# Convolution and gate kernel on one core: in blocks 27 to 33 the product of chunk 2 goes from VectorE to GpSimd, with ScalarE evicting it first

## The chip, the cores and the metric

The kernel runs on one core of one Trainium2 chip. The metric is the time of one execution on the device, in microseconds; the time of before is the median of three runs.

A core has five engines that run their own queues of instructions strictly in order and wait for each other with semaphores: TensorE (PE, with its weight loads as PEld) for matrix products, VectorE (DVE), ScalarE (ACT) and GpSimd (POOL) for elementwise work, and SyncE (SP), which here only issues DMAs. TensorE writes to PSUM; here VectorE and ScalarE read it from there.

## What is computed

```python
def _attn_ref(x, weight):                 # x (8, 4224, 192), weight (8, 7)
    w = softmax(weight, axis=-1)          # one 7-tap filter per head, 8 heads of 24 channels
    # causal convolution along the sequence, one filter for the 24 channels of a head
    out = np.einsum('hk,bskhg->bshg', w, x_unf)

def _moe_ref(x, w_val, conv_w, w_out):    # x is the result above
    for k in range(5):                    # causal, one 5-tap filter for each channel
        gate_pre += conv_w[k][None, None, :] * xp[:, k:k + S, :]
    gate = 1.0 / (1.0 + np.exp(-gate_pre))
    val = x @ w_val                       # 192 x 192
    return gate * val @ w_out             # 192 x 192
```

## The kernel before, in words

**Layout.** The eight sequences are laid end to end as two halves of four. Channels lie on the partitions and tokens on the free axis. 192 channels are one and a half times 128 partitions, so three chunks are worked on: chunks 0 and 1 are the first 128 channels of the two halves of the batch, held together as one tile with 2 x 502 columns, and chunk 2 is the other 64 channels of both halves, stacked into 128 partitions, 502 columns.

**Groups and blocks.** The tokens are cut into 14 groups (NJS), and the groups into 36 blocks (STEPS, numbered n = 0 to 35). Most blocks have 502 tokens of each half; blocks 32 and 33 have 448, block 34 has 500 and block 35 has 188. The last block of the loop, n = 36, only finishes block 35.

**The first convolution** is a product with a banded matrix on TensorE. Its work is cut into units (`conv_unit`): four matrix products into one PSUM bank (pc, L318), one copy by ScalarE (e, L327), and, where a head is complete, DMAs on SP's queue that scatter the result into the group's x tiles (L356) and issue the next loads of the input (L167). Units are run two groups ahead: the list `todo` says how many units run at the end of each block. Group 12 (blocks 32 and 33) and group 13 (blocks 34 and 35) are the last.

**A block** has these steps, in the shorthand of the code:

- `split(n+1)`: x of the next block is split into a rounded part and a remainder, since TensorE multiplies rounded values. ScalarE casts (xh, L418 for chunks 0 and 1, L426 for chunk 2) and GpSimd subtracts (xl, L419 and L427).
- v = x @ w_val on TensorE, in parts: `diagonal` (L453), `main` (L463), `columns` (L491), `rows` (L476). Chunk 2 of v is finished by `columns`, chunks 0 and 1 by `rows`.
- the gate of a coming block. For chunks 0 and 1 together (tile pa) and for chunk 2 (tile pb), ScalarE opens an accumulator in PSUM with the first tap (`gate_open`, L390), VectorE adds taps 1 to 4 one after the other (`gate_taps`, L397), and ScalarE closes it with the sigmoid (`gate_close`, L410) into the tile g. There is one accumulator for each, so the next block's opening comes right after the closing.
- `gated(n, q)`: g times v for chunk q, from the PSUM bank of v, in place in g (L510, VectorE).
- `split_gated1(n)` and `split_gated2(n)`: the product is split again for the second matrix product: ScalarE casts (ph), GpSimd subtracts (pl).
- o = (g v) @ w_out, one block behind: the products of block n-1 are made during block n, and `project(n-1, q)` copies each bank out (ot, L526) to be stored.

**PSUM.** The accumulators of the gate have banks of their own. All else, v, o and pc, takes five banks in turn (pool `ps`). In a block the order of taking is v chunk 2, o chunk 2, v chunk 0, v chunk 1, o chunk 0, o chunk 1, then one for each unit of the convolution. So o chunk 1 takes the bank of v chunk 2 of the same block; it can start when that is read.

**The order of the work** is written out by hand: every engine runs its instructions in the order of the calls. The main loop (L636 to L675) calls the steps above. VectorE's taps are the part that can be shifted: a block must have done a number of them (`ahead(n)`) ahead of its own gate, eight per block plus a lead that the table LEAD gives (4 taps in blocks 19 to 27, then 3, 2, 1 and 0). Taps ahead of `gated(n, 2)` are here called the first part, those that the second `while` adds, up to a cost of FITS, the second. When the last tap of an accumulator is done, `flush` puts its closing and the next opening on ScalarE's queue: at the next tap of the same kind, or at one of the calls of `flush` in the loop. If the last tap of chunks 0 and 1 falls in the second part, up to two convolution units are put ahead of that closing.

Of the kernel before, what the change touches and what calls it, by code (L numbers as in the profile page):

```python
# [7 lines left out]
F32 = mybir.dt.float32  # L8
# [4 lines left out]
ALU = mybir.AluOpType  # L13
# [47 lines left out]
NG = len(NJS)  # L61
# [7 lines left out]
STEPS = []  # L69
# [5 lines left out]
N = len(STEPS)  # L75
LAST = N - 1
MB = 502
# [19 lines left out]

LEAD = {0: 0, 10: 1, 13: 2, 16: 3, 19: 4, 28: 3, 30: 2, 32: 1, 33: 0}  # L100
BETWEEN = {9, 12, 15, 18}
COST, FITS = (1.3, 0.78), 4.6

SOON = {2: (0, 2), 3: (1, 3), 4: (3, 5), 5: (5, 8)}

# [2 lines left out]
def kernel(  # L108
# [9 lines left out]
    nc = tc.nc  # L118
# [5 lines left out]
    gp = ctx.enter_context(tc.tile_pool(name="gp", bufs=3))  # L124
    pp = ctx.enter_context(tc.tile_pool(name="pp", bufs=2))
    op = ctx.enter_context(tc.tile_pool(name="op", bufs=3))
    ps_g = ctx.enter_context(tc.tile_pool(name="ps_g", bufs=1, space=PSUM))
    ps_h = ctx.enter_context(tc.tile_pool(name="ps_h", bufs=1, space=PSUM))
    ps = ctx.enter_context(tc.tile_pool(name="ps", bufs=5, space=PSUM))
# [51 lines left out]
    def scratch(n, i):  # L181
        o = scr_at[i]
        scr_at[i] += n
        return scr[i][:, o : o + n].bitcast(I32)

    raw = {}
    for name, ap, n, i in (("wv", wv, 2 * D + 2 * KG, 2), ("wo", wo, 2 * D, 1)):
        t = scratch(2 * n, i)
# [182 lines left out]
    def views(n, k=KG - 1):  # L371
        g, o, m = STEPS[n]
        b = second(NJS[g])
        x1v = x1s[g][:, : 2 * b].rearrange("p (a t) -> p a t", a=2)
        return x1v[:, :, o + k : o + k + m], x2s[g][:, o + k : o + k + m]
# [3 lines left out]
    accs, g1s, g2s, xs, pr, ots, banks = {}, {}, {}, {}, {}, {}, {}  # L379

    def gate_open(n, i):
        if n >= N:
            return
        m = STEPS[n][2]
        if i == 0:
            acc = ps_g.tile([128, 2, 512], F32, tag="pa", name=f"pa_{n}")[:, :, :m]
        else:
            acc = ps_h.tile([128, 512], F32, tag="pb", name=f"pb_{n}")[:, :m]
        accs[n, i] = acc
        nc.scalar.mul(acc, views(n, 0)[i], cwt[:, i, 0:1])  # L390
# [11 lines left out]
    def gate_close(n, i):  # L402
        if n >= N:
            return
        m = STEPS[n][2]
        if i == 0:
            dst = g1s[n] = gp.tile([128, 2, MB], F32, tag="g1", name=f"g1_{n}")[:, :, :m]
        else:
            dst = g2s[n] = gp.tile([128, MB], F32, tag="g2", name=f"g2_{n}")[:, :m]
        nc.scalar.activation(dst, accs.pop((n, i)), AF.Sigmoid)  # L410
# [11 lines left out]
    def split2(pool, tag, n, x):  # L422
        m = STEPS[n][2]
        h = pool.tile([128, MB], F32R, tag="h2", name=f"{tag}h2_{n}")[:, :m]
        l = pool.tile([128, MB], F32R, tag="l2", name=f"{tag}l2_{n}")[:, :m]
        nc.scalar.copy(h, x)  # L426
        nc.gpsimd.tensor_tensor(out=l, in0=x, in1=h.bitcast(F32), op=ALU.subtract)  # L427
        return h, l
# [3 lines left out]
    def bank(what, n, q):  # L432
        t = ps.tile([128, 512], F32, tag="p", name=f"{what}_{n}_{q}")[:, : STEPS[n][2]]
        banks[what, n, q] = t
        return t

    def operands(what, n):
        return (w_val, *xs[n, 1], *xs[n, 2]) if what == "v" else (w_out, *pr[n, 1], *pr[n, 2])

    def parts(w, h, l):  # L440
        return (w.h, h), (w.l, h), (w.h, l)

    def ok(n):
        return 0 <= n < N

    def diagonal(what, n):
        if not ok(n):
            return
        acc = bank(what, n, 2)
        w, _, _, h2, l2 = operands(what, n)  # L450
        r = slice(W22, W22 + 128)
        for i, (a, b) in enumerate(parts(w, h2, l2)):
            nc.tensor.matmul(acc, lhsT=a[:, r], rhs=b, start=(i == 0), stop=False)  # L453

    def main(what, n, q):
        if not ok(n):
            return
        fresh = (what, n, q) not in banks
        acc = bank(what, n, q) if fresh else banks[what, n, q]
        w, h, l, _, _ = operands(what, n)  # L460
        r = slice(W11, W11 + 128)
        for i, (a, b) in enumerate(parts(w, h, l)):
            nc.tensor.matmul(  # L463
                acc, lhsT=a[:, r], rhs=b[:, q], start=(fresh and i == 0), stop=(not fresh and i == 2)
            )

    def rows(what, n):
        if not ok(n):
            return
        fresh = (what, n, 0) not in banks  # L470
        two = [bank(what, n, q) if fresh else banks[what, n, q] for q in range(2)]
        w, _, _, h2, l2 = operands(what, n)
        r = slice(W21, W21 + 128)
        for i, (a, b) in enumerate(parts(w, h2, l2)):
            for acc, p in zip(two, HALVES):
                nc.tensor.matmul(  # L476
                    acc, lhsT=a[p, r], rhs=b[p], start=(fresh and i == 0), stop=(not fresh and i == 2)
                )

    def columns(what, n):  # L480
        if not ok(n):
            return
        m = STEPS[n][2]
        acc = banks[what, n, 2]
        w = w_val if what == "v" else w_out
        x = views(n)[0] if what == "v" else g1s[n]
        cuts = [m * i // 4 for i in range(5)]
        for i in range(4):
            c = slice(cuts[i], cuts[i + 1])
            for q, p in enumerate(HALVES):  # L490
                nc.tensor.matmul(  # L491
                    acc[p, c], lhsT=w.f[:, W12 : W12 + 64], rhs=x[:, q, c],
                    start=False, stop=(i == 3),
                )

    def split(n):
        if n >= N:
            return
        x1, x2 = views(n)
        if n == 0:  # L500
            xs[n, 2] = split2(sp, "x", n, x2)
        xs[n, 1] = split1(sp, "x", n, x1)
        if n > 0:
            xs[n, 2] = split2(sp, "x", n, x2)

    def gated(n, q):
        if not ok(n):
            return
        v = g1s[n][:, q] if q < 2 else g2s[n]
        nc.vector.tensor_tensor(out=v, in0=banks.pop(("v", n, q)), in1=v, op=ALU.mult)  # L510

    def split_gated1(n):
# [3 lines left out]
    def split_gated2(n):  # L516
        if ok(n):
            pr[n, 2] = split2(pp, "p", n, g2s[n])

    def project(n, q):  # L520
        if not ok(n):
            return
        m = STEPS[n][2]
        if n not in ots:
            ots[n] = op.tile([128, 3 * MB], F32, tag="ot", name=f"ot_{n}")
        nc.scalar.copy(ots[n][:, q * m : (q + 1) * m], banks.pop(("o", n, q)))  # L526
        o = 3 * sum(s[2] for s in STEPS[:n])
        if n == LAST:
            nc.sync.dma_start(out[:, o + q * m : o + (q + 1) * m], ots[n][:, q * m : (q + 1) * m])
        elif q == 1:  # L530
            nc.sync.dma_start(out[:, o : o + 3 * m], ots[n][:, : 3 * m])
# [16 lines left out]
    for g in range(LAG, NG):  # L548
        a, b = SOON.get(g) or (first[g - LAG], first[g - 1])
        if g == NG - 1:  # L550
            a, b = a - 1, b - 1
        k = first_unit[g + 1] - first_unit[g]
        for i in range(k):
            todo[a + i * (b - a) // k] += 1
# [63 lines left out]
    def flush(*which):  # L618
        for n, i in [p for p in pending if p[1] in which]:
            gate_close(n, i)  # L620
            gate_open(n + 1, i)
            pending.remove((n, i))
# [9 lines left out]
    def ahead(n):  # L632
        lead = LEAD[max(k for k in LEAD if k <= n)]
        return min(2 * T * (n - HEAD) + T + lead, len(taps))

    for n in range(HEAD, N + 1):  # L636
        diagonal("v", n)
        split(n + 1)
        diagonal("o", n - 1)
        main("v", n, 0)  # L640
        main("v", n, 1)
        while at_tap[0] < ahead(n):
            tap()
        columns("v", n)
        gated(n, 2)
        flush(0)
        columns("o", n - 1)
        split_gated2(n)
        project(n - 1, 2)
        rows("v", n)  # L650
        if n in BETWEEN:
            tap()
        gated(n, 0)
        gated(n, 1)
        rows("o", n - 1)
        split_gated1(n)
        flush(1)
        main("o", n - 1, 0)
        used = first_used = 0
        while at_tap[0] < ahead(n + 1):  # L660
            _, i, k = taps[at_tap[0]]
            if used + COST[i] > FITS:
                break
            used += COST[i]
            tap()
            if (i, k) == (0, T):
                first_used = used
        project(n - 1, 0)
        main("o", n - 1, 1)
        project(n - 1, 1)  # L670
        now = min(todo[n], 2 if first_used else 0)
        conv(now)
        flush(0)
        conv(todo[n] - now)
        flush(1)  # L675
# [91 lines left out]
```

## Time and profile before

| What | Value |
|---|---|
| Median of 3 runs | 390.35 us (389.66 to 391.41) |
| Profiled execution | 390.87 us |
| Its span in the profile | 388.7 us |
| TensorE busy | 375.8 us, 97% of the span |
| VectorE busy | 340.8 us, 88% |
| ScalarE busy | 327.4 us, 84% |
| GpSimd busy | 254.6 us, 66% |
| Granted TensorE clock, mean | 0.992 |

The profile is of one execution. Its span lies a little below that execution's own time, the rest being what lies around the traced instructions. Rows that group instructions give the line, the engine, the operation, what is written from what, the number of instructions, and then busy time in us, the mean in ns of one, and the idle time of the engine just before them with what ended it. Rows of the order of time give the start in us, the length in us, the engine, the line and the operation; in brackets stands how long the engine had been idle and what it had waited for. Where instructions of one engine overlap a little, the distance of two starts is what one of them costs.

### The profile page before, as it was taken

How to read it: one execution, taken by the hardware profiler on the slowest of the kernel's cores; microseconds unless marked ns; L12 is line 12 of the kernel's file. 1: busy time of each engine (PE TensorE's matmuls, PEld its weight loads, DVE VectorE, ACT ScalarE, POOL GpSimd, SP SyncE). 2: the span in 40 equal slices, each digit the busy share in tenths (PEclk: the TensorE clock that was granted, in tenths of full speed). 3: DMA queues.
4: the chain of work that ended last, by engine and by line, in shares of the span. 5: the costliest groups of instructions: out<-in, count | busy, mean ns of one | idle time of the engine just before them, and what ended most of it. 6: DMA issues, size and time to landing. Idle time of an engine off the chain costs nothing.

```text
span 388.7 us, 8631 instructions
## 1 busy us (share of the span) xinstructions
PE 375.8 (97%) x3204; PEld 321.0 (83%) x3204; DVE 340.8 (88%) x424; ACT 327.4 (84%) x525; POOL 254.6 (66%) x177
## 2 busy tenths in 40 slices
PE   8798999999999999999999999999999999999895
PEld 8697988988888888888888888888888788887784
DVE  4769899888999999999999999899899988999970
ACT  7568888989888889889988988888888889987863
POOL 1869765556667765666665766776566675777771
PEclk9989999999999999999999999999999999999998
DMA  8887869999788689687867668768887736342223
GB/s 297 235 207 228 249 216 288 255 271 223 227 247 237 197 244 230 211 236 239 244 197 237 201 193 257 206 198 260 249 234 209 242 128 215 124 147 80 81 103 149
DMA packets 38209, 82.49 MB, mean 212 GB/s; under 512 B 4856, under 2 KB 17528, under 8 KB 38168
## 3 DMA queue, kind: packets, MB, share of 16 engines
q1 hardware_dynamic: 36720, 79.90, 68.4%
q0 software_dynamic: 896, 1.31, 1.4%
q10 hardware_dynamic: 552, 0.73, 0.6%
q8 instruction: 25, 0.41, 0.5%
q14 instruction: 16, 0.13, 0.1%
HBM read 29.34 MB, written 26.00 MB: 142 GB/s over the span
## 4 chain that ended last, share of the span: by engine, by line
PE 86%; DVE 6%; DMA 3%; ACT 2%; issue 1%; SPq 1%; DVEq 0%; ACTq 0%
PE pc L318 22%; PE o L463 13%; PE v L463 11%; PE v L491 8%; PE v L476 7%; PE o L491 7%; PE o L476 6%; PE o L453 5%; PE v L453 5%; DVE pa L397 3%; DVE g L510 2%; DMA x<-xw 2%; DVE pb L397 1%; PE pw L210 1%; SPq L356 1%
## 5 line engine op out<-in xcount | busy, mean ns | idle before, releaser
L397 DVE SCALAR_TENSOR_TENSOR pa<-x,cwt,pa 128x1004 f32<-128x1004 f32 (+5 forms) x144 | 172.8, 1200 | 9.5 <-ACT pa L390 5.6
L419 POOL TENSOR_TENSOR xl<-x,xh 128x1004 fp32r<-128x1004 f32 (+5 forms) x36 | 74.7, 2075 | 80.3 <-ACT xh L418 69.1
L318 PEld LDWEIGHTS pc<-band,x 128*120 128x120 f32 x912 | 102.8, 187 | 5.8 <-issue 3.4
L318 PE MATMUL pc<-band,x 128*120 128x122 f32 x912 | 103.8, 272 | 3.2 <-DMA x<-xw 3.2
L397 DVE SCALAR_TENSOR_TENSOR pb<-x,cwt,pb 128x502 f32<-128x502 f32 (+5 forms) x144 | 102.2, 710 | 3.9 <-ACT pb L390 0.7
L419 POOL TENSOR_TENSOR pl<-g,ph 128x1004 fp32r<-128x1004 f32 (+5 forms) x36 | 79.1, 2197 | 21.4 <-ACT ph L418 19.2
L510 DVE TENSOR_TENSOR g<-v,g 128x502 f32<-128x502 f32 (+5 forms) x108 | 65.8, 642 | 21.0 <-PE v L476 16.4
L327 ACT COPY e<-pc 120x488 f32<-120x488 f32 x114 | 61.3, 576 | 13.0 <-PE pc L318 11.9
L526 ACT COPY ot<-o 128x502 f32<-128x502 f32 (+5 forms) x108 | 55.9, 547 | 3.3 <-PE o L463 2.6
L427 POOL TENSOR_TENSOR pl<-g,ph 128x502 fp32r<-128x502 f32 (+5 forms) x36 | 43.4, 1204 | 13.4 <-ACT ph L426 13.1
L418 ACT CAST ph<-g 128x1004 fp32r<-128x1004 f32 (+5 forms) x36 | 35.2, 979 | 14.7 <-DVE g L510 14.6
L410 ACT ACTIVATE g<-pa 128x1004 f32<-128x1004 f32 (+5 forms) x36 | 34.7, 965 | 10.7 <-DVE pa L397 9.9
L427 POOL TENSOR_TENSOR xl<-x,xh 128x502 fp32r<-128x502 f32 (+5 forms) x36 | 41.8, 1161 | 0.0
L390 ACT ACTIVATE pa<-x,cwt 128x1004 f32<-128x1004 f32 (+5 forms) x36 | 37.8, 1050 | 2.5 <-DMA x<-e 1.4
L491 PEld LDWEIGHTS v<-x,wvf 128*64 128x64 f32 x576 | 29.1, 136 | 11.8 <-issue 11.4
L491 PE MATMUL v<-x,wvf 128*64 128x125 f32 (+4 forms) x576 | 37.2, 270 | 0.0
L491 PE MATMUL o<-g,wof 128*64 128x125 f32 (+4 forms) x576 | 35.5, 264 | 0.0
L418 ACT CAST xh<-x 128x1004 fp32r<-128x1004 f32 (+5 forms) x36 | 35.2, 978 | 0.0
L491 PEld LDWEIGHTS o<-g,wof 128*64 128x64 f32 x576 | 30.9, 136 | 0.1
L463 PE MATMUL o<-ph,woh 128*128 128x502 f32 (+5 forms) x72 | 30.9, 429 | 0.0
L463 PE MATMUL v<-xh,wvh 128*128 128x502 f32 (+5 forms) x72 | 27.2, 377 | 0.3 <-ACT e L327 0.3
L463 PE MATMUL o<-ph,wol 128*128 128x502 f32 (+5 forms) x72 | 27.2, 377 | 0.0
(75 smaller groups left out, 567.4 us busy)
## 6 DMA issues: line engine op xcount, KB each, us to landing
x<-xw SPq DMA_DIRECT2D x64, 300.0 KB
out<-ot SPq DMA_DIRECT2D x24, 753.0 KB
x<-e SPq DMA_DIRECT2D x40, 285.9 KB
x<-xw SPq DMA_DIRECT2D x20, 360.0 KB
out<-ot SPq DMA_DIRECT2D x8, 672.0 KB
x<-e SPq DMA_DIRECT2D x32, 141.6 KB
x<-e SPq DMA_DIRECT2D x25, 171.6 KB
x<-e SPq DMA_DIRECT2D x16, 94.4 KB
```

Source lines behind the costliest of these rows:

```text
L318: nc.tensor.matmul(pc[:M, k * WIN : (k + 1) * WIN], lhsT=xtiles[i][:, c : c + M], rhs=band[:, 4 * q + hi, :], start=True, stop=True,)
L327: nc.scalar.copy(e[:, a : a + w], pc[:M, :w])
L397: nc.vector.scalar_tensor_tensor(out=acc, in0=views(n, k)[i], scalar=cwt[:, i, k : k + 1], in1=acc, op0=ALU.mult, op1=ALU.add,)
L418: nc.scalar.copy(h, x)
L419: nc.gpsimd.tensor_tensor(out=l, in0=x, in1=h.bitcast(F32), op=ALU.subtract)
L427: nc.gpsimd.tensor_tensor(out=l, in0=x, in1=h.bitcast(F32), op=ALU.subtract)
L453: nc.tensor.matmul(acc, lhsT=a[:, r], rhs=b, start=(i == 0), stop=False)
L463: nc.tensor.matmul(acc, lhsT=a[:, r], rhs=b[:, q], start=(fresh and i == 0), stop=(not fresh and i == 2))
L476: nc.tensor.matmul(acc, lhsT=a[p, r], rhs=b[p], start=(fresh and i == 0), stop=(not fresh and i == 2))
L491: nc.tensor.matmul(acc[p, c], lhsT=w.f[:, W12 : W12 + 64], rhs=x[:, q, c], start=False, stop=(i == 3),)
L510: nc.vector.tensor_tensor(out=v, in0=banks.pop(("v", n, q)), in1=v, op=ALU.mult)
L526: nc.scalar.copy(ots[n][:, q * m : (q + 1) * m], banks.pop(("o", n, q)))
```

## The change

Four things change. In blocks 27 to 33 (ASIDE) chunk 2's product is made by GpSimd: ScalarE copies the bank of v into a new tile in SBUF (vt, one buffer), and GpSimd multiplies it with g. In these blocks the call of `gated(n, 2)` moves behind `flush(0)`, and the call of `split_gated2(n)` moves behind `project(n-1, 2)`. The lead is five taps in blocks 27 to 31, three in block 32 and none from block 33. And group 12's six units run in blocks 26 and 27, three each, where they ran in blocks 26, 27 and 28, two each; block 28 keeps the two units of group 13.

```diff
-LEAD = {0: 0, 10: 1, 13: 2, 16: 3, 19: 4, 28: 3, 30: 2, 32: 1, 33: 0}
+LEAD = {0: 0, 10: 1, 13: 2, 16: 3, 19: 4, 27: 5, 32: 3, 33: 0}
+
+ASIDE = range(27, N - 2)
...
+    vp = ctx.enter_context(tc.tile_pool(name="vp", bufs=1))
...
         v = g1s[n][:, q] if q < 2 else g2s[n]
+        if q == 2 and n in ASIDE:
+            t = vp.tile([128, MB], F32, tag="vt", name=f"vt_{n}")[:, : STEPS[n][2]]
+            nc.scalar.copy(t, banks.pop(("v", n, q)))
+            nc.gpsimd.tensor_tensor(out=v, in0=t, in1=v, op=ALU.mult)
+            return
         nc.vector.tensor_tensor(out=v, in0=banks.pop(("v", n, q)), in1=v, op=ALU.mult)
...
         if g == NG - 1:
             a, b = a - 1, b - 1
+        if g == NG - 2:
+            b = b - 1
...
         columns("v", n)
-        gated(n, 2)
+        if n not in ASIDE:
+            gated(n, 2)
         flush(0)
+        if n in ASIDE:
+            gated(n, 2)
         columns("o", n - 1)
-        split_gated2(n)
+        if n not in ASIDE:
+            split_gated2(n)
         project(n - 1, 2)
+        if n in ASIDE:
+            split_gated2(n)
         rows("v", n)
```

With the new leads, the taps by block are as follows (28a4 is the fourth tap of block 28's chunks 0 and 1, 28b1 the first of its chunk 2):

```
block  first part                     second part
27     28a4 28b1-28b4 29a1            29a2 29a3 29a4
28     29b1-29b4 30a1                 30a2 30a3 30a4
29     30b1-30b4 31a1                 31a2 31a3 31a4
30     31b1-31b4 32a1                 32a2 32a3 32a4
31     32b1-32b4 33a1                 33a2 33a3 33a4
32     33b1-33b3                      33b4 34a1 34a2
33     34a3 34a4                      34b1-34b4 35a1
```

Before, block 27 had 28a4 28b1-28b4 and then 29a1-29a3, block 28 had 29a4 29b1-29b3 and then 29b4 30a1 30a2, and so on, so that the last tap of chunks 0 and 1 always stood in the first part.

## The prediction

> **What bounds the kernel now.** I read the page first (busy shares and the chain that ended last), then the stretches block by block, then each engine's order of time in blocks 27 to 35.
>
> ```profile
> span 388.7 us, 8631 instructions
> PE 375.8 (97%) x3204; PEld 321.0 (83%) x3204; DVE 340.8 (88%) x424; ACT 327.4 (84%) x525; POOL 254.6 (66%) x177
> PE 86%; DVE 6%; DMA 3%; ACT 2%; issue 1%; SPq 1%; DVEq 0%; ACTq 0%
> ```
>
> TensorE sets the time, and it stops doing so only where VectorE carries 6% of the chain. A block starts at its first diagonal product of v; cut at these starts, blocks 26 to 34 are:
>
> ```profile
> 293.75:303.18 9.43, 9.43 (x81) 7.80 (x80) 8.81 (x11) 8.18 (x13) 5.83 (x5) 1.00 0.87 248
> 303.18:313.54 10.36, 9.94 (x82) 7.87 (x80) 10.11 (x13) 9.19 (x15) 7.51 (x5) 1.00 0.58 187
> 313.54:324.66 11.12, 11.12 (x98) 9.47 (x96) 10.14 (x12) 9.47 (x15) 7.68 (x5) 1.00 0.56 194
> 324.66:334.15 9.49, 9.49 (x82) 7.84 (x80) 8.09 (x11) 8.53 (x13) 5.57 (x4) 1.00 0.41 125
> 334.15:343.55 9.40, 9.40 (x82) 7.79 (x80) 8.82 (x11) 8.61 (x14) 6.91 (x5) 1.00 0.39 139
> 343.55:351.63 8.08, 8.08 (x66) 6.29 (x65) 7.69 (x11) 7.05 (x11) 5.75 (x4) 1.00 0.47 163
> 351.63:360.15 8.52, 7.83 (x64) 6.08 (x62) 8.37 (x11) 6.87 (x12) 6.31 (x4) 1.00 0.23 91
> 360.15:368.66 8.51, 7.43 (x64) 6.01 (x62) 8.34 (x10) 6.58 (x12) 6.49 (x5) 1.00 0.23 93
> 368.66:376.10 7.44, 7.44 (x64) 6.07 (x63) 6.54 (x12) 5.38 (x11) 5.71 (x5) 1.00 0.23 92
> ```
>
> The columns are the length, then busy time of PE, PEld, DVE, ACT and POOL, the granted clock (1.00 throughout) and the DMAs. A block with two convolution units is 9.43 us of PE work (26, 29, 30); four units make 11.12, so a unit is 0.84. Block 27 has two units and takes 10.36: 0.93 lost. Block 31, without units, should take 9.40 - 1.68 = 7.72 and takes 8.08: 0.36. Blocks 32 and 33 do no more than block 34 (7.44) and take 1.08 and 1.07 longer. That is 3.4 us, and the rows say who has it:
>
> ```profile
> 309.58 0.49 PE L476 MATMUL o<-ph,woh 64*128 64x502 f32 x1 [0.42 <-DVE g L510]
> 357.82 0.49 PE L476 MATMUL o<-ph,woh 64*128 64x502 f32 x1 [0.69 <-DVE g L510]
> 366.52 0.47 PE L476 MATMUL o<-ph,woh 64*128 64x448 f32 x1 [1.08 <-DVE g L510]
> ```
>
> The second accumulator of "rows o" takes the PSUM bank of v chunk 2, which VectorE frees only when its queue reaches `gated(n, 2)`. This is what the change attacks.
>
> **The change, part by part.** *VectorE loses* seven products:
>
> ```profile
> L510 DVE TENSOR_TENSOR g<-v,g 128x502 f32<-128x502 f32 x72 | 46.5, 675 | 12.1 <-PE v L476 11.6 <-PE v L491 0.4
> L427 POOL TENSOR_TENSOR pl<-g,ph 128x502 fp32r<-128x502 f32 x24 | 30.6, 1277 | 7.7 <-ACT ph L426 7.4
> L427 POOL TENSOR_TENSOR xl<-x,xh 128x502 fp32r<-128x502 f32 x24 | 29.0, 1210 | 0.0
> L419 POOL TENSOR_TENSOR pl<-g,ph 128x1004 fp32r<-128x1004 f32 x24 | 55.9, 2329 | 16.4 <-ACT ph L418 14.8 <-DMA x<-e 0.6 <-PE o L463 0.6
> L419 POOL TENSOR_TENSOR xl<-x,xh 128x1004 fp32r<-128x1004 f32 x24 | 51.6, 2148 | 60.8 <-ACT xh L418 55.8 <-DMA x<-e 5.0
> ```
>
> 7 x 0.675 = 4.7 us off VectorE's queue, which was what PE waited for. With PE bound everywhere the most this can return is the 3.4 us above. *The convolution units* only move: block 26 gets a third (starting 27 at 303.18 + 0.84 = 304.02), block 27 a third, block 28 drops to two. The sum for PE is 0, and so is that of their copies and scatter DMAs; these leave SP's queue earlier. Their cover is PE's work on other blocks' data; if a scatter landed late it would cost the wait of ScalarE's opening for block 32, at the earliest one block later, so I take 0.
>
> *ScalarE and GpSimd gain* seven copies and seven products, and here the order matters more than the sum. In an ASIDE block ScalarE's queue is: cast xh, cast xh2 (block n+1); copy of v; one output copy; **cast ph2, which needs GpSimd's product**; cast ph; close and open of chunk 2; two output copies; two convolution copies; close and open of chunks 0 and 1; next block's xh. GpSimd's is: xl, xl2 (they need xh, xh2), **product**, pl2, pl. So cast ph2 waits until GpSimd has done xl, xl2 and the product, these wait for cast xh, and the next cast xh is behind cast ph2. That is a closed loop, once round per block; before, ph2 waited for VectorE and no loop ran through GpSimd. Its price, from block 28 (times are starts; the distance of two starts is the cost):
>
> ```profile
> 313.83 1.05 ACT L327 COPY e<-pc 120x488 f32<-120x488 f32 x2
> 314.75 1.06 ACT L418 CAST xh<-x 128x1004 fp32r<-128x1004 f32 x1
> 315.68 0.64 ACT L426 CAST xh<-x 128x502 fp32r<-128x502 f32 x1
> 316.19 1.04 ACT L410 ACTIVATE g<-pa 128x1004 f32<-128x1004 f32 x1
> 317.26 1.10 ACT L390 ACTIVATE pa<-x,cwt 128x1004 f32<-128x1004 f32 x1
> 318.61 0.61 ACT L426 CAST ph<-g 128x502 fp32r<-128x502 f32 x1 [0.24 <-DVE g L510]
> 319.13 0.57 ACT L526 COPY ot<-o 128x502 f32<-128x502 f32 x1
> 320.68 1.03 ACT L418 CAST ph<-g 128x1004 fp32r<-128x1004 f32 x1 [0.98 <-DVE g L510]
> 321.62 1.05 ACT L526 COPY ot<-o 128x502 f32<-128x502 f32 x2
> 322.56 1.26 ACT L327 COPY e<-pc 120x488 f32<-120x488 f32 x2
> ...
> 325.39 0.60 ACT L410 ACTIVATE g<-pb 128x502 f32<-128x502 f32 x1
> 326.02 0.69 ACT L390 ACTIVATE pb<-x,cwt 128x502 f32<-128x502 f32 x1
> 326.64 1.02 ACT L418 CAST xh<-x 128x1004 fp32r<-128x1004 f32 x1
> ```
>
> ```profile
> 315.89 2.15 POOL L419 TENSOR_TENSOR xl<-x,xh 128x1004 fp32r<-128x1004 f32 x1 [1.66 <-ACT xh L418]
> 318.00 1.28 POOL L427 TENSOR_TENSOR xl<-x,xh 128x502 fp32r<-128x502 f32 x1
> 319.36 1.28 POOL L427 TENSOR_TENSOR pl<-g,ph 128x502 fp32r<-128x502 f32 x1
> ```
>
> GpSimd's leg: 314.75 to 315.89 is 1.14 from xh's start to xl's, xl 2.11, xl2 1.28, the product 1.28 (not in the trace; the same width and operand count as xl2), 0.05 of hand-over: 5.86. The copy of v (0.57 by the output copies' row) and two neighbours hide in it; uncovered, seven copies would cost 4.0. ScalarE's leg: ph2 0.52, ph 0.94, close 0.63 and open 0.62, two output copies 0.94, two convolution copies 0.92, close 1.07, open 1.10: 6.74. Once round: **12.6 us, against 9.43 of PE work.**
>
> The lead belongs to this sum. With the leads of before, the last tap of chunk 0 falls ahead of the gate, and its close and open (2.17) run while GpSimd is at xl. With five taps it falls after the convolution copies, so both stand in ScalarE's leg, ahead of the next cast xh; queued behind them are the two casts and everything GpSimd does.
>
> The older limit of before is that xh starts at block start plus 1.2 (314.75 - 313.54). PE can stand a lag only until it needs the next bank: with two units the next diagonal product of o takes the bank of o chunk 0, freed by an output copy 5.86 + 0.52 + 0.94 + 1.25 + 0.57 = 9.1 after xh's start. PE wants it 9.43 + 0.7 = 10.1 after the block's start. So the slack is used up when xh starts 1.0 into the block; every further turn of the loop is paid in full.
>
> **The sum.** The casts xh by block, from these rows:
>
> ```profile
> 304.91 1.06 ACT L418 CAST xh<-x 128x1004 fp32r<-128x1004 f32 x1
> ...
> 346.50 2.11 POOL L419 TENSOR_TENSOR xl<-x,xh 128x896 fp32r<-128x896 f32 x1 [1.70 <-DMA out<-ot]
> 348.56 1.16 POOL L427 TENSOR_TENSOR xl<-x,xh 128x448 fp32r<-128x448 f32 x1
> ...
> 371.52 0.49 ACT L418 CAST xh<-x 128x376 fp32r<-128x376 f32 x1
> ```
>
> Block 27: 304.91 + 0.46 (a third convolution copy of block 26) = 305.37. Its leg through GpSimd ends at 311.23; ScalarE's 6.74 and a third convolution copy (0.46) bring xh of block 28 to 318.43, which is 4.1 into a block that starts at 304.02 + 10.3 = 314.3. From there 12.6 each for blocks 28 and 29, and 12.4 for block 30, whose close and opens are already of 448: 331.0, 343.6, 356.0. Block 31 has no convolution copies and narrower x: GpSimd 1.0 + 2.06 + 1.16 + 1.28 + 0.05 = 5.55, ScalarE 6.74 - 0.92 - 0.25 = 5.57, together 11.1: 367.1. In blocks 32 and 33 fewer taps are ahead, and chunk 0's close and open are out of ScalarE's leg: 5.45 + 3.45 = 8.9 and 5.85 + 3.2 = 9.05 (outputs of 448): 385.0 for the cast that was at 371.52. Block 34 is gated by VectorE again, and the rest runs as before. The lag is 385.0 - 371.5 = 13.5 us.
>
> The profiled execution took 390.87 (span 388.7), 0.52 over the median of the runs, 390.35. 390.87 + 13.5 = 404.4, on the median's footing **403.9**. A shift of this kind already holds VectorE's gain: with PE and ScalarE late, VectorE is never late.
>
> *Bounds.* Product at VectorE's own price (0.675), xl2 at its mean (1.21): the loop is 11.9, and six such turns take 4 off: 400. Product 8% dearer, as pl stands to xl among the wide rows (2329 to 2148), and 0.14 for each hand-over, as 319.36 stands to the end of cast ph2 (318.61 + 0.61): 0.4 a turn, 2.5 more: 406.5. I take 1.28, as GpSimd's two-input subtractions at that width all lie between 1.21 and 1.28 on the group rows.
>
> [...]
>
> **The rivals.**
> (a) *Faster.* The loop doesn't bite and the VectorE waits vanish: 390.35 - 3.4 = 387.0. It needs ScalarE's ph2 to find the product ready, so GpSimd to be through xl and xl2 before v is. For it: GpSimd is busy only 5.6 to 7.7 us a block. Against it: the order of the queues; share of busy time says nothing of a loop. It decides where a turn is below 9.43, 3.2 less than the rows give.
> (b) *Half of it.* PE's slack and shorter legs take part of the lag, turns of about 11: 404 - 6 x 1.5 = 395. For it: the 5-bank rotation can reach further than I walked. Against: the slack was 0 in block 28 already.
> (c) *No change.* ScalarE's extra 4.0 us replaces VectorE's 3.4 us as a plain load: 391.
> (d) *Clock.* PE idles about 2.3 us at a time (block 29: at 324.5 + 0.7 against a bank freed near 327.5); if the clock fell, the 9.43 of PE work would double in places and join the loop: 408 to 415. Against: 1.08 us of wait left the granted clock at 1.00 in block 33, and nothing longer stands in these blocks.
> [...]
>
> **How the numbers follow.** My forecast 0.74, (a) 0.08, (b) 0.09, (c) 0.04, (d) 0.05. What a measurement here can tell is about 0.5%, 2 us. Faster is (a), 0.08; same is (c), 0.04; the rest, 0.88, is slower. The range 396 to 410 takes my forecast with both bounds, the upper half of (b) and the start of (d).
>
> **What would show it.** Right: ScalarE's cast ph2 (L426) waits 2 to 3 us for the new GpSimd product in blocks 28 to 31; xh to xh is about 12.5 us there; PE waits for ScalarE's output copies at the diagonal product of o (L453), not for L510. Blocks 26 and before are unchanged but for one unit. Wrong: GpSimd's product starts as soon as the copy of v lands, xh stays near 1.2 us into its block, or block lengths stay near 9.4.

## The result, and the profile after

The changed kernel takes 401.9 us (median of 6 runs, 400.36 to 403.76); the kernel before takes 389.6 us in the same comparison. The ratio is 1.0303, with a 95% interval of 1.0273 to 1.0332: 12.3 us slower, where 13.5 were forecast. The profiled execution took 403.76 us with a span of 402.0, 13.3 more than the span before.

The page of the changed kernel: span and busy times, and the shares of the chain that ended last.

```profile
span 402.0 us, 8617 instructions
PE 381.9 (95%) x3204; PEld 322.8 (80%) x3204; DVE 337.6 (84%) x417; ACT 330.0 (82%) x532; POOL 262.6 (65%) x184
PE 74%; POOL 8%; issue 7%; ACT 4%; DMA 3%; DVE 2%; SPq 1%; POOLq 0%; DVEq 0%; ACTq 0%
```

VectorE has seven instructions and 3.2 us less, and its share of the chain fell from 6% to 2%, as the change means it to. But GpSimd, which had no share, now has 8%, ScalarE 4%, and TensorE fell from 86% to 74%. No engine is busier than before as a share of the span. In microseconds TensorE is: 6.1 more for the same 3204 products, in part because its granted clock is 0.87 and 0.85 in two of the blocks below. But that is not what sets the time there: from 320.15 to 383.12 us the chain runs through GpSimd and ScalarE alone. Its "issue", up from 1% to 7%, stands in large part where GpSimd waits for ScalarE's cast xh (3.46 us from 329.03, for example).

Stretches of the changed kernel, blocks 27 to 33, cut at the first diagonal product of v (length, then busy time of PE, PEld, DVE, ACT, POOL, granted clock, DMAs):

```profile
304.80:315.25 10.45, 10.45 (x89) 8.79 (x87) 10.14 (x12) 9.21 (x16) 7.60 (x6) 1.00 0.67 211
315.25:325.05 9.80, 9.80 (x81) 7.88 (x79) 8.72 (x11) 6.51 (x11) 5.56 (x4) 1.00 0.50 171
325.05:338.47 13.42, 11.29 (x82) 8.87 (x80) 8.92 (x10) 10.50 (x17) 8.76 (x6) 0.87 0.25 85
338.47:349.53 11.06, 10.18 (x82) 7.79 (x80) 9.43 (x12) 7.76 (x14) 7.35 (x5) 1.00 0.33 117
349.53:361.19 11.66, 9.61 (x65) 7.14 (x64) 6.56 (x9) 8.65 (x15) 8.01 (x5) 0.85 0.33 113
361.19:370.89 9.70, 8.49 (x63) 5.84 (x62) 7.57 (x10) 7.72 (x12) 6.76 (x5) 1.00 0.20 79
370.89:381.19 10.30, 7.98 (x64) 5.86 (x62) 6.74 (x8) 7.32 (x12) 8.94 (x7) 1.00 0.19 76
```

The seven blocks take 76.4 us. Before they took 65.5 (303.18 to 368.66), and 64.6 without the unit that now runs in block 26. So 11.8 of the 13.3 us lie here; 0.8 was there already when block 27 began (304.80, where 303.18 + 0.84 = 304.02 stood in the sum), and 0.8 comes after block 33. The first 0.8 has nothing to do with the change: this execution is that much later than the one of before from 24 us on (24.63 against 23.87 for the same diagonal product). Block 27 is whole, block 28 nearly so, and every block from 29 on pays.

The order of time of ScalarE in the changed kernel, block 28 and the beginning of block 29, shows the queue going through the loop:

```profile
319.05 1.02 ACT L421 CAST xh<-x 128x1004 fp32r<-128x1004 f32 x1
319.97 0.61 ACT L429 CAST xh<-x 128x502 fp32r<-128x502 f32 x1
320.48 0.58 ACT L515 COPY vt<-v 128x502 f32<-128x502 f32 x1
...
324.80 0.61 ACT L429 CAST ph<-g 128x502 fp32r<-128x502 f32 x1 [3.26 <-POOL g L516]
325.31 1.03 ACT L421 CAST ph<-g 128x1004 fp32r<-128x1004 f32 x1
...
331.44 1.01 ACT L421 CAST xh<-x 128x1004 fp32r<-128x1004 f32 x1
```

And GpSimd in the same stretch:

```profile
320.15 2.16 POOL L422 TENSOR_TENSOR xl<-x,xh 128x1004 fp32r<-128x1004 f32 x1 [3.95 <-PE o L494]
322.27 1.27 POOL L430 TENSOR_TENSOR xl<-x,xh 128x502 fp32r<-128x502 f32 x1
323.50 1.26 POOL L516 TENSOR_TENSOR g<-vt,g 128x502 f32<-128x502 f32 x1
325.49 1.26 POOL L430 TENSOR_TENSOR pl<-g,ph 128x502 fp32r<-128x502 f32 x1 [0.72 <-ACT ph L429]
326.70 2.33 POOL L422 TENSOR_TENSOR pl<-g,ph 128x1004 fp32r<-128x1004 f32 x1
332.52 2.16 POOL L422 TENSOR_TENSOR xl<-x,xh 128x1004 fp32r<-128x1004 f32 x1 [3.50 <-ACT xh L421]
```

The copy of v has landed at 321.06 and GpSimd could multiply; it is at xl and xl2 until 323.5. ScalarE stands for 3.26 us at cast ph2, then does the rest of the block, and only at 331.44 comes to the cast that GpSimd has been waiting for, 3.5 us long. Each engine waits for the other once in a turn. (The first xl's wait is put down to a product of TensorE; it starts 0.08 us after cast xh ends.) The waits of the changed kernel from 303 us to 399 us add up to this (engine, line, for whom: total, times, longest):

```profile
ACT ph L429 <- POOL g L516: 17.4, 7, 3.3
POOL xl L422 <- ACT xh L421: 15.2, 6, 3.5
...
DVE g L518 <- PE v L479: 13.3, 8, 3.4
...
PE o L456 <- ACT ot L534: 5.1, 3, 2.1
```

TensorE meets the loop where its bank comes free late:

```profile
328.10 0.49 PE L456 MATMUL o<-ph,woh 128*128 128x502 f32 x1 [2.13 <-ACT ot L534]
340.28 0.49 PE L456 MATMUL o<-ph,woh 128*128 128x502 f32 x1 [0.88 <-ACT ot L534]
352.51 0.50 PE L456 MATMUL o<-ph,woh 128*128 128x502 f32 x1 [2.06 <-ACT ot L534]
```

These are the diagonal products of o in blocks 29 to 31. The waits of "rows o" for VectorE, which were the target, are gone; in blocks 32 and 33 waits of 0.48 and 0.78 us for ScalarE's copy of v stand in their place. There TensorE also waits for cast ph2 (0.99 us, block 33) and for pl2 (0.61 and 0.56).

### The profile page after: what moved, and what is told of

It reads as the page before. It is cut to its first block, busy times and chain, and to the rows that moved or that the text cites. A ratio compares the mean times of both kernels' runs of the same rounds, so it can differ in the third digit from the quotient of the medians.

```text
span 402.0 us, 8617 instructions
## 1 busy us (share of the span) xinstructions
PE 381.9 (95%) x3204; PEld 322.8 (80%) x3204; DVE 337.6 (84%) x417; ACT 330.0 (82%) x532; POOL 262.6 (65%) x184
## 4 chain that ended last, share of the span: by engine, by line
PE 74%; POOL 8%; issue 7%; ACT 4%; DMA 3%; DVE 2%; SPq 1%; POOLq 0%; DVEq 0%; ACTq 0%
PE pc L321 21%; PE o L466 11%; PE v L466 9%; PE v L494 7%; PE o L494 6%; PE v L479 6%; PE o L479 5%; PE o L456 5%; PE v L456 4%; POOL pl L422 2%; POOL g L516 2%; DMA x<-xw 2%; POOL xl L430 2%; POOL pl L430 1%; ACT ph L429 1%
## 5 line engine op out<-in xcount | busy, mean ns | idle before, releaser
L400 DVE SCALAR_TENSOR_TENSOR pa<-x,cwt,pa 128x1004 f32<-128x1004 f32 (+5 forms) x144 | 172.8, 1200 | 12.4 <-ACT pa L393 8.6
L518 DVE TENSOR_TENSOR g<-v,g 128x502 f32<-128x502 f32 (+5 forms) x101 | 61.5, 641 | 31.6 <-PE v L479 25.7
L421 ACT CAST ph<-g 128x1004 fp32r<-128x1004 f32 (+5 forms) x36 | 35.2, 978 | 12.3 <-DVE g L518 12.3
L429 ACT CAST ph<-g 128x502 fp32r<-128x502 f32 (+5 forms) x36 | 20.9, 579 | 24.1 <-POOL g L516 17.4
L494 PEld LDWEIGHTS v<-x,wvf 128*64 128x64 f32 x576 | 30.2, 140 | 12.3 <-issue 12.2
L494 PE MATMUL v<-x,wvf 128*64 128x125 f32 (+4 forms) x576 | 38.4, 276 | 0.0
```

What stands on the lines that cost most here:

```text
L400: nc.vector.scalar_tensor_tensor(out=acc, in0=views(n, k)[i], scalar=cwt[:, i, k : k + 1], in1=acc, op0=ALU.mult, op1=ALU.add,)
L494: nc.tensor.matmul(acc[p, c], lhsT=w.f[:, W12 : W12 + 64], rhs=x[:, q, c], start=False, stop=(i == 3),)
```

## The experiments

The theory: a turn of the loop (cast xh, xl, xl2, product, cast ph2, the rest of ScalarE's block, the next cast xh) is longer than TensorE's block, and the difference is the loss. The rivals: the moved units; the longer lead by itself; the added load of ScalarE and GpSimd; the price of a product on GpSimd. Every ratio below is against the kernel before, run beside it; the changed kernel's is 1.0303.

**The units alone.**

```diff
         if g == NG - 1:
             a, b = a - 1, b - 1
+        if g == NG - 2:
+            b = b - 1
```

> Only group 12's units move to blocks 26 and 27; leads and products as before. The loop theory (cast ph2 waits for GpSimd's product, which waits for the next block's cast xh and its two differences) expects the time of before, 389.6 within 1 us, since the work of TensorE is the same and no wait is new. A theory that the earlier units crowd ScalarE or the scatter queue expects 392 or more, with blocks 26 and 27 longer than their 10.3 us of products.

Measured: 389.24 us, ratio 1.0005 (0.9981 to 1.0029). The moved units cost and bring nothing that can be told.

**All but the product.** The changed kernel with an empty ASIDE: leads and units as changed, chunk 2 gated by VectorE in all blocks.

```diff
-ASIDE = range(27, N - 2)
+ASIDE = ()
```

> The changed kernel's leads and units, but chunk 2's product stays on VectorE in every block. The loop theory expects 388 to 391: no loop, VectorE still short of time in blocks 28 to 33. A theory that the longer lead itself costs the time, since chunk 0's closing and opening come late on ScalarE, expects 395 to 402.

Measured: 389.36 us, ratio 1.0012 (0.9988 to 1.0035). The longer lead by itself costs nothing that can be told. TensorE's waits only move: 0.94 us in block 27, where one tap more than before stands ahead of VectorE's product, and 0.88 for xl2 at the start of block 33.

**The load without the wait.** Two forms. In the first VectorE makes the real product, ScalarE copies the same bank, and GpSimd multiplies the copy with itself into a tile that nobody reads.

```diff
-            nc.scalar.copy(t, banks.pop(("v", n, q)))
-            nc.gpsimd.tensor_tensor(out=v, in0=t, in1=v, op=ALU.mult)
...
+            acc = banks.pop(("v", n, q))
+            nc.vector.tensor_tensor(out=v, in0=acc, in1=v, op=ALU.mult)
+            nc.scalar.copy(t, acc)
+            nc.gpsimd.tensor_tensor(out=u, in0=t, in1=t, op=ALU.mult)
```

> The changed kernel's order, with ScalarE's copy of v and a GpSimd product of the same size in blocks 27 to 33, but the product goes to a tile that nobody reads; VectorE makes the real one. So ScalarE and GpSimd carry the whole new load and only the wait of cast ph2 for GpSimd is gone. The loop theory expects 389 to 392 and no wait of cast ph2 above 1.5 us. A theory that the added load (0.5 us of ScalarE and 1.27 us of GpSimd a block) makes these engines the bound expects about 400.

Measured: 394.18 us, ratio 1.0144 (1.0103 to 1.0185), outside what the theory expected. The trace says why this was no clean trial. The copy now waits for VectorE's product on the same bank (first row: 4.9 us in five times), a wait that the changed kernel doesn't have. The bank comes free later still, and in block 27 TensorE stands for 1.53 us and then runs at half its clock (granted 0.50 from 312 to 314 us, the stretch below). The row names VectorE; ScalarE's copy of that bank ends at 310.25, 0.03 before TensorE goes on. How much of the loss each of these makes is not shown. GpSimd's product with twice the same input took 1.03 us here, less than the real one (1.26 in the changed kernel). From the waits, the order of time and a stretch of this run:

```profile
ACT vt L518 <- DVE g L517: 4.9, 5, 1.9
...
310.28 0.55 PE L479 MATMUL o<-ph,woh 64*128 64x502 f32 x1 [1.53 <-DVE g L521]
...
312.00:314.00 2.00, 2.00 (x6) 1.56 (x6) 1.94 (x2) 1.85 (x4) 2.00 (x2) 0.50 0.73 248
```

So I repeated it on data that nobody fights over: VectorE makes chunk 2's product at its old place, ScalarE copies o's chunk 2 bank a second time, right behind its first copy, and GpSimd multiplies that.

```diff
+        acc = banks.pop(("o", n, q))
...
+        if q == 2 and n + 1 in ASIDE:
...
+            nc.scalar.copy(t, acc)
+            nc.gpsimd.tensor_tensor(out=u, in0=t, in1=ots[n][:, q * m : (q + 1) * m], op=ALU.mult)
```

> The changed kernel's leads, units and order, VectorE making chunk 2's product; in blocks 27 to 33 ScalarE copies o's chunk 2 bank a second time and GpSimd multiplies that copy with the output tile into a tile that nobody reads. The same load on ScalarE and GpSimd as in the changed kernel, at the same place of their queues, with no engine waiting for VectorE or for the product because of it. The loop theory expects 389 to 392, near the 389.4 of the run without a product on GpSimd. If the load alone makes ScalarE or GpSimd the bound, about 400; in between, the load has that share.

Measured: 390.68 us, ratio 1.0032 (1.0009 to 1.0055), 0.8 us over the run without the load by the ratios, with intervals that meet. The same work at the same place of the queues costs about a fifteenth of the loss when cast ph2 doesn't wait for it. What there is of it shows as TensorE waiting for pl2 (3.0 us in three times, in the short blocks).

**One tap less.** The changed kernel with a lead of four in blocks 27 to 31.

```diff
-LEAD = {0: 0, 10: 1, 13: 2, 16: 3, 19: 4, 27: 5, 32: 3, 33: 0}
+LEAD = {0: 0, 10: 1, 13: 2, 16: 3, 19: 4, 32: 3, 33: 0}
```

> The changed kernel with four taps of lead in blocks 27 to 31 where it has five. The closing and opening of chunks 0 and 1 then lie ahead of the gate, beside GpSimd's xl, and leave ScalarE's part of the loop: 12.4 - 2.1 = 10.3 a turn in blocks 28 to 30, about 9 in block 31. The loop theory expects 390 to 394, eight or more of the twelve us gone. A theory that the product on GpSimd is too slow in itself, or that the added load is the bound, expects it to stay near 400.

Measured: 393.53 us, ratio 1.0094 (1.0064 to 1.0123). Eight of the twelve us are gone with one tap. Its casts xh:

```profile
316.92 1.07 ACT L421 CAST xh<-x 128x1004 fp32r<-128x1004 f32 x1
327.26 1.06 ACT L421 CAST xh<-x 128x1004 fp32r<-128x1004 f32 x1
337.36 1.06 ACT L421 CAST xh<-x 128x1004 fp32r<-128x1004 f32 x1
347.61 0.97 ACT L421 CAST xh<-x 128x896 fp32r<-128x896 f32 x1
356.67 0.95 ACT L421 CAST xh<-x 128x896 fp32r<-128x896 f32 x1
```

Turns of 10.34, 10.10, 10.25 and 9.06 us in blocks 28 to 31, where 10.3 and 9 were expected and the changed kernel has 12.39, 12.09, 12.14 and 11.01. Without the product the fifth tap costs nothing that can be told, and with it 8: the two act together, because the tap moves 2.1 us of ScalarE's work into the loop. No rival that counts one or the other alone gives this.

**A longer turn, and the same work outside it.** A second GpSimd product, once ahead of the real one and once behind pl.

Inside:

```diff
             nc.scalar.copy(t, banks.pop(("v", n, q)))
...
+            nc.gpsimd.tensor_tensor(out=u, in0=t, in1=v, op=ALU.mult)
             nc.gpsimd.tensor_tensor(out=v, in0=t, in1=v, op=ALU.mult)
```

Outside:

```diff
             pr[n, 1] = split1(pp, "p", n, g1s[n])
+            if n in ASIDE:
...
+                nc.gpsimd.tensor_tensor(out=u, in0=ts[n], in1=g2s[n], op=ALU.mult)
```

> The changed kernel with a second GpSimd product of the same size into a tile nobody reads, just ahead of the real one. It stands inside the loop: 1.2 us a turn, six to seven turns, so the loop theory expects 401.9 + 7.5 to 8.5 = 409 to 411. A theory in which the loss is in TensorE's clock or in single late waits expects 2 us or less.

> The same extra product, but behind pl at the end of GpSimd's block, where GpSimd was idle for 2.3 to 3.5 us in blocks 28 to 31. It is outside the loop: the loop theory expects 401 to 403.5, within 1.5 us of the changed kernel. If GpSimd's sum of work is the bound, it costs the same 8 us as inside.

Measured: inside 411.32 us, ratio 1.0551 (1.0505 to 1.0598), 2.5 points over the changed kernel, or 9.7 us, and a little above the 409 to 411 expected; outside 403.46 us, ratio 1.0354 (1.0303 to 1.0406), whose interval meets the changed kernel's. Casts xh inside the loop, blocks 28 to 31:

```profile
318.98 1.02 ACT L421 CAST xh<-x 128x1004 fp32r<-128x1004 f32 x1
332.70 1.01 ACT L421 CAST xh<-x 128x1004 fp32r<-128x1004 f32 x1
346.10 1.01 ACT L421 CAST xh<-x 128x1004 fp32r<-128x1004 f32 x1
359.57 0.92 ACT L421 CAST xh<-x 128x896 fp32r<-128x896 f32 x1
```

13.72, 13.40 and 13.47 a turn, 1.3 more each than the changed kernel, where 1.2 were expected. With the product outside, the turns are the changed kernel's (319.15 to 331.55, 12.40):

```profile
319.15 1.03 ACT L421 CAST xh<-x 128x1004 fp32r<-128x1004 f32 x1
331.55 1.01 ACT L421 CAST xh<-x 128x1004 fp32r<-128x1004 f32 x1
```

GpSimd does the same work in both. What counts is whether it stands between cast xh and cast ph2.

**The product first.** In blocks 27 to 33 the split of the next x is called behind the gate, so that GpSimd's queue is product, xl, xl2, pl2, pl.

```diff
-        split(n + 1)
+        if n not in ASIDE:
+            split(n + 1)
...
         if n in ASIDE:
             gated(n, 2)
+            split(n + 1)
```

> The changed kernel, but in blocks 27 to 33 the split of the next block's x is called behind the gate of chunk 2, so that GpSimd's queue is product, xl, xl2, pl2, pl. Cast ph2 then waits only for the copy of v and one product, and the loop through xl and xl2 is open. The loop theory expects 386.5 to 390, block lengths near 9.45 in blocks 28 to 30 and cast ph2 waiting under 0.5 us. If GpSimd's product is too slow or too crowded in itself, the time stays above 395.

Measured: 393.85 us, ratio 1.0119 (1.009 to 1.0147), above the 386.5 to 390 expected and half right. Blocks 28 to 30 run as expected (starts of diagonal products at 314.36, 323.79, 333.31, 342.71: 9.43, 9.52, 9.40), so the loop is open there. But in blocks 31 to 33, which have no units, xl2 now comes too late for the diagonal product of v of the block behind:

```profile
352.00 0.48 PE L456 MATMUL v<-xl,wvh 128*128 128x448 f32 x1 [0.78 <-POOL xl L430]
360.90 0.47 PE L456 MATMUL v<-xl,wvh 128*128 128x448 f32 x1 [0.71 <-POOL xl L430]
371.34 0.49 PE L456 MATMUL v<-xl,wvh 128*128 128x500 f32 x1 [1.96 <-POOL xl L430]
```

**Two versions from this.** One keeps all seven products on GpSimd, product first in blocks 27 to 30 and between xl and xl2 in 31 to 33, with leads of four in block 32 and one in block 33 (its edit is below); the other gives the product to GpSimd in blocks 27 to 30 alone, product first, and sets the leads from there to 5, 2 and 0.

```diff
-LEAD = {0: 0, 10: 1, 13: 2, 16: 3, 19: 4, 27: 5, 32: 3, 33: 0}
+LEAD = {0: 0, 10: 1, 13: 2, 16: 3, 19: 4, 27: 5, 32: 4, 33: 1, 34: 0}
...
 ASIDE = range(27, N - 2)
+FIRST, MIDDLE = range(27, 31), range(31, N - 2)
...
-        split(n + 1)
+        if n not in FIRST:
+            split(n + 1, (1,) if n in MIDDLE else (1, 2))
...
-        if n not in ASIDE:
+        if n not in FIRST:
             gated(n, 2)
+        if n in MIDDLE:
+            split(n + 1, (2,))
         flush(0)
-        if n in ASIDE:
+        if n in FIRST:
             gated(n, 2)
+            split(n + 1)
```

> All seven products of chunk 2 stay on GpSimd, but the loop is cut short everywhere: in blocks 27 to 30 GpSimd's queue is product, xl, xl2, pl2, pl as in the run with the product first; in blocks 31 to 33, which have no convolution units and are shorter, it is xl, product, xl2, pl2, pl, since xl2 behind all of them came 0.7 to 2.0 us late for the next block there, and the copy of v stands ahead of the closing of chunks 0 and 1. Leads: 5 in blocks 27 to 31, 4 in 32, 1 in 33. The loop theory expects block lengths of 9.45 in 28 to 30 and 7.8, 7.5 and 7.2 in 31 to 33, which leaves about 2.5 of the 3.4 us that VectorE cost: 386.5 to 388.5. If the added load is a bound in itself, 390 or more.

Measured: 391.04 us, ratio 1.0035 (1.0007 to 1.0064), a miss. Blocks 32 and 33 still take 9.35 and 8.89 us, and TensorE waits 0.64 and 1.06 us for xl2 at their starts. The waits of this run, and block 32:

```profile
ACT ph L430 <- POOL g L518: 4.0, 2, 2.1
POOL xl L423 <- ACT xh L422: 3.4, 3, 1.9
...
348.16:357.51 9.35, 8.40 (x63) 5.84 (x62) 7.84 (x11) 7.76 (x12) 7.42 (x6) 1.00 0.21 82
```

It is the loop again. In this order xl and the product still stand between cast xh and cast ph2, and cast ph2 waits for the product twice. With a lead of five in block 31 the closing and opening of chunks 0 and 1 are in ScalarE's part too. The casts xh of blocks 31 and 32 stand at 343.84 and 353.76, a turn of 9.92 us, where these blocks have 7.4 to 7.7 us of TensorE work. GpSimd's load is no bound in block 32: it works 7.42 of the 9.35 us and stands for 1.93 us before the xl at 354.77. In block 33 it works 8.58 of 8.89 us; whether its load alone would hold that block is not shown.

> The product goes to GpSimd only in blocks 27 to 30, ahead of the differences; from block 31 VectorE makes it as before, with leads 5, 2 and 0. The loop theory expects block 27 and 31 to lose nothing and blocks 32 and 33 to lose about as much as before (VectorE short by 1 to 2 us): 387.5 to 389, that is up to 0.4% faster. If any product on GpSimd costs time in these blocks, 390 or more.

Measured: 388.15 us against 388.82, ratio 0.9969 (0.9946 to 0.9993): 0.3% faster than the kernel before, as expected, though the interval nearly reaches 1. Its blocks 27 to 33:

```profile
303.97:314.26 10.29, 10.29 (x90) 8.61 (x88) 10.08 (x12) 9.50 (x16) 5.92 (x5) 1.00 0.69 219
314.26:323.68 9.42, 9.42 (x81) 7.76 (x80) 8.35 (x10) 8.92 (x15) 7.33 (x6) 1.00 0.52 176
...
342.62:350.58 7.96, 7.96 (x65) 6.21 (x64) 7.48 (x10) 6.83 (x11) 6.77 (x5) 1.00 0.48 165
350.58:358.25 7.67, 7.67 (x64) 5.90 (x63) 6.48 (x10) 7.23 (x12) 5.33 (x3) 1.00 0.25 101
358.25:366.87 8.62, 7.54 (x64) 5.75 (x63) 7.75 (x9) 6.75 (x12) 8.62 (x7) 1.00 0.23 91
```

62.9 us for the seven, 1.7 less than before without the moved unit. Block 27 loses nothing and block 32 little; block 33 still loses what it did. No run has these leads without the products, so what each brings is not shown.

## Why the prediction was right, point by point

**The loop and its price.** Right. The casts xh of the changed kernel stand at 306.16, 319.05, 331.44, 343.53, 355.67, 366.68, 375.50 and 384.43. Turns, forecast and measured: 13.06 and 12.89 (block 27), 12.6 and 12.39, 12.6 and 12.09, 12.4 and 12.14, 11.1 and 11.01, 8.9 and 8.82, 9.05 and 8.93. All are a little short, 79.7 against 78.3 in sum, so the loop took 1.4 us less than forecast; with the late start of 0.8 the last of these casts lags 12.9 us behind the 371.52 of before, where 13.5 were forecast. Without that late start, which this execution brought along, the lag is 12.1, beside the 12.3 of the medians. The mis-sized terms: the opening of chunks 0 and 1 costs 1.04 ahead of another cast (330.40 to 331.44), where I took its whole length of 1.10; in block 29 it is already one of 896 columns and costs 0.95 (342.58 to 343.53), and xl2 there cost 1.03 (334.64 to 335.67) for 1.28. The sign that I named is there: cast ph2 waits 3.26, 2.50, 3.24 and 2.30 us for the product in blocks 28 to 31, where I wrote 2 to 3.

**The product's own price.** 1.25 to 1.30 us at 502 columns (1.26 in the rows above), where I took 1.28.

**The lead belongs to the sum.** Right: one tap is 2.05 us a turn (12.39 to 10.34, forecast 2.17) and 8 us in all.

**What hides what.** Right for the loop: the copy of v was costed at nothing, beside GpSimd's leg, and it runs at 320.48 while GpSimd is at xl. That TensorE would wait for this copy in blocks 32 and 33 (0.48 and 0.78 us) I did not see; the chain doesn't pass there. The moved units were costed at nothing: ratio 1.0005. VectorE was never to be late, and is not: by the waits above it waits 13.3 us itself, for "rows" of v.

**How far TensorE can stand the lag.** I wrote that the slack is gone once xh starts 1.0 us into its block, and put the first wait at the diagonal product of o in block 29 at 2.3 us. It is there, 2.13 us, and behind ScalarE's output copy. "The rest runs as before" was a little too much: block 34 takes 8.31 us (381.19 to 389.50) where it took 7.4.

**The rivals.** (a) needed a turn below 9.43; in blocks 28 to 30 the shortest with seven products was 10.1, until the order of GpSimd's queue was changed. (b) fell with the turns. (c), the load alone, is 0.8 us by the second of the two load runs, with intervals that meet. (d), the clock, was put too low as an event: I argued from 1.08 us of wait without a fall that waits of 2.3 would do no harm, and the clock did fall after waits of 2.13 and 2.06 (last section). Its price was small here, since ScalarE and GpSimd, not TensorE, set the turn: in block 29, with the clock at 0.87, the turn was 12.09, the shortest of the long ones, and the chain has no piece of TensorE there.

What stays open: the six executions of the changed kernel spread over 3.4 us, wider than those of before within this comparison (2.5), and only the longest is traced. Its mean granted clock is the lowest of the six, 0.982; the two shortest have 0.991, but one of 402.54 us has 0.992. How much the clock weighs in the other five is not shown.

## What to carry to other kernels

When work is handed to another engine, follow the queues around: if its result goes back to an engine that also feeds it, in order, there is a loop, and its turn (the sum of what stands between, on both engines) is a floor on the block, whatever the shares of busy time say. Here a product outside that path cost nothing that could be told, and the same product in it its full length, 1.3 us a turn. So look first at the order of one queue: it opened the loop in blocks 28 to 30 without taking any work away. A longer lead doesn't shorten such a loop; here it lengthened it by 2.1 us a turn, by moving other work into it.

## What the runs showed of the hardware that was not expected

In the changed kernel TensorE's clock fell to half for some 3 us (granted 0.50 from 330 to 332 us, and from 354 to 356) after single waits of 2.13 and 2.06 us, where I had argued from a wait of 1.08 us without a fall that none would come. Stretches of the changed kernel around the wait that ended at 328.10:

```profile
327.00:329.00 2.00, 0.90 (x4) 0.78 (x5) 1.39 (x2) 2.00 (x5) 2.00 (x1) 1.00 0.00 0
329.00:331.00 2.00, 2.00 (x7) 1.18 (x5) 1.59 (x3) 1.97 (x3) 0.03 (x1) 0.60 0.85 337
331.00:333.00 2.00, 2.00 (x21) 1.94 (x22) 1.27 (x1) 1.96 (x3) 0.47 (x1) 0.54 0.63 178
333.00:335.00 2.00, 2.00 (x26) 1.64 (x24) 0.13 (x1) 1.16 (x2) 2.00 (x2) 1.00 0.21 56
```

The wait itself is still granted 1.00 here; the fall shows from 329 us on, about one us behind it. In blocks 27 to 34 of the traces such a fall followed waits of 1.53 us (the first load run), 1.96 (product first), 2.06 and 2.13 (the changed kernel), 2.13 (the extra product outside the loop), and 2.40 and 3.46 (inside it). None followed the waits up to 1.43 us there. But the length of the single wait doesn't decide it alone: with the extra product outside a wait of 2.04 us was not followed by a fall, and with it inside, waits of 2.02, 2.21 and 3.32 were not (the last row here is the stretch behind the longest of these). What else does is not shown.

```profile
356.42 0.50 PE L456 MATMUL o<-ph,woh 128*128 128x502 f32 x1 [3.32 <-ACT ot L536]
...
358.00:360.00 2.00, 2.00 (x28) 1.61 (x28) 1.05 (x3) 1.97 (x3) 0.00 (x0) 1.00 0.95 329
```

In the first load run the loss did not end with the wait: after its 1.53 us, products of 502 columns stood 0.42 us apart at the granted clock of 0.50 (312.18, 312.60, 313.01), where at 1.00 they stood 0.22 and 0.23 apart a little later (316.91, 317.13, 317.36).
